# A leaner opening of an S4 and gMLP kernel: shorter table arithmetic, small transfers ahead of large ones, constant bf16 products on TensorE

## The chip, the core and the metric

The kernel runs on one core of a Trainium2 chip. The metric is the device time of one execution in microseconds (us). In the profile PE is TensorE (PEld its weight loads), DVE is VectorE, ACT is ScalarE, POOL is GpSimd and SP is SyncE.

## The reference

One token stream x of 2048 x 576 goes through two sublayers, each behind a layernorm that the conditioning vector c modulates:

```python
mod = (silu(c) @ w_mod).reshape(1, 6, 1, 576)   # w_mod: 576 x 3456
sa, ca, ga, sb, cb, gb = (mod[:, i] for i in range(6))
h = layernorm(x) * (1 + ca) + sa
x = x + ga * S4(h)
h = layernorm(x) * (1 + cb) + sb
x = x + gb * gMLP(h)
```

S4 is a long convolution, one per channel: dt = exp(log_dt), K[d, l] = Re(sum over n of C[d, n] dt B[d, n] exp(dt A[d, n] l)) for 576 channels, 128 states and 2048 positions, then y = conv(K, h) + h * Dskip. gMLP is z = gelu(h @ w_in) with 4608 columns, the second half layernormed and multiplied along the positions by w_sp (2048 x 2048, plus b_sp), the product of both halves times w_out.

## The kernel before, in words

`body` calls `ssm` (modulation, first layernorm, S4) and then the two phases of the MLP, whose start `ssm` also weaves in. The change concerns the first fifth of `ssm`.

Per pole (one channel and state) the kernel needs the logarithm of C B dt as a magnitude (`lw`) and a phase in turns (`ph`), the decay `al` = dt A_re, and the turns per position `tau` with its 64-fold `tau64`, both without their whole turns. `poles` makes these as tables: `p0` for the first 128 channels, 128 x 144 elements, and `p1` for the other 384 of its four groups, 128 x 432. Each of the five results is split into three bf16 parts (`split3`: two copies on ACT, two differences on DVE, into `pt`), which POOL's queue writes to DRAM (`pa_d`, `pb_d`). `poles_load` reads them back rearranged, so that the parts lie along the partitions: `lb` holds the parts of al and lw, `lc` and `la` those of tau, tau64 and ph. Against the constant matrix `sel` TensorE then makes exponents (`e_unit`: lb x sel into a double bank ps and a bank pk, exponentiated by ACT into `et`) and phases (`t_unit`: lc and la x sel into ps; DVE takes the absolute value and ACT two sines, into `ft`). `p_unit` multiplies both on DVE into `pg`, `kg_unit` multiplies the pieces of the kernel K on TensorE (evicted by ACT into `kab`), `k1_unit` takes a first step of the convolution's transform. These units run for g = 0, 1, 2, ..., 35.

Beside this stand the modulation and the layernorm. `mod_unit(k)` multiplies one of the six parts of w_mod with silu(c) (the tile `ec`): 6 small f32 products for each half of the columns into two banks, evicted by ACT into `mpart`; a product with a matrix of ones (a part of the tile `small`) sums the partial results and spreads them over all partitions. k = 2 gives `gar` (ga), k = 1 gives `cga` = (1 + ca) ga, k = 0 gives `sga` = sa ga, which goes through three bf16 copies `gsp` with two corrections on DVE between them. The w_mod parts arrive as `wm`, `k_a` and `k_b`. `ln_stats(i)` makes the mean and 1/std of one of four tiles of x (`ln_x`, four blocks of 128 rows each): tiles 0 and 1 by copies and squares with accumulation on ACT (into a junk tile `st1o`, sums in `nm` and `ss`), tiles 2 and 3 by BATCH_NORM_STATS2 on DVE (`bs`). `ln_rows(b)` centres and scales block b with cga and makes `rt`, a constant rotation times 1/std. `ln_half(k)`, for sixteen half pairs of blocks, multiplies rows by rotations and adds gsp x `cs` into four banks; ACT evicts these to `st1o`, and POOL stores them (`u_d`).

The order of everything is written by hand. Every instruction of every engine is issued through `Pin.call`, which pins it behind the one before on its engine; so nearly all rows of the profile have its line, L223. The table `ORDER` (L53 on) is a list of tokens: a letter for the unit and a number for its instance. The class `Steps` (L880) runs the tokens: the units are generators, and each token runs one to its next `yield`. B are set-up steps (B0 starts the p0 loads, B1 those of p1, B2 to B6 load c, sel, small, msk and dsk, B7 the first part of w_mod), O a step of p0, P a step of p1, M a step of a `mod_unit`, i, w loads of w_mod, j, x loads of ln_x, g, r, a loads of the rotations, S `ln_stats`, R `ln_rows`, A `ln_half`, Q `poles_load`, and e, t, p, k and 1 the units above. `PLAN` names the buffer of each use of the ring tiles: five of `et`, three of `ft`, four banks pk_a to pk_d, two double banks ps_a and ps_b, and so on. A bank pk has 512 f32 columns; the modulation and `ln_half` use 288 of them (HC), `kg_unit` and `k1_unit` 256.

## Time and profile before

| | |
|---|---|
| three runs | 1691.30, 1702.78, 1696.13 us; median 1696.13 |
| profiled execution | 1701.01 us, span 1698.9 |
| busy: PE, PEld | 1623.6 (96%), 1239.8 us |
| busy: DVE, ACT, POOL | 1298.9 (76%), 875.5 (52%), 210.6 us |
| mean granted TensorE clock | 0.98 of full speed |
| DMA | 380.61 MB, 224 GB/s over the span |

The span runs from the first to the last instruction of the record. A row of a timeline has a start, a duration, the engine, the operation, out<-in by the program's names, and in brackets the idle time ahead of it with what ended it. A row of the stretches has a window, its length and the busy time of each engine in it with the count of instructions. A row of the groups has the total busy time, the mean of one in ns, and the idle time ahead of them. PEclk is the TensorE clock that was granted, as a share of full speed; rows at half speed show 0.50.

### The profile page before, as it was taken

Reading aid. Unit: us, or ns where it says so; the run is one execution under the profiler, and the core shown is the slowest. Engines: PE = TensorE matmul, PEld = TensorE weight load, DVE = VectorE, ACT = ScalarE, POOL = GpSimd, SP = SyncE. Lnnn points to the kernel's source line nnn. Section 1 sums busy time; section 2 is a strip of 40 time slices with the busy share of each in tenths; the row PEclk is TensorE's granted clock in tenths of the full one; section 3 lists DMA queues with packets and bytes.
Section 4 is the critical chain, followed back from the end, with each engine's and each line's share of the span. In section 5 each row is a group of like instructions: output and inputs, shape, how many; then the busy total and the mean of one; then the engine's idle time right before and its main releaser. Section 6 shows DMA issues by size and latency. Waiting matters only on the chain.

```text
span 1698.9 us, 39926 instructions
## 1 busy us (share of the span) xinstructions
PE 1623.6 (96%) x16870; PEld 1239.8 (73%) x16870; DVE 1298.9 (76%) x2241; ACT 875.5 (52%) x1309; POOL 210.6 (12%) x340
## 2 busy tenths in 40 slices
...
GB/s 231 168 206 214 189 147 177 180 285 222 264 289 240 256 266 289 254 258 247 244 127 284 304 265 253 228 210 173 225 224 233 194 233 119 263 282 251 192 243 29
DMA packets 186386, 380.61 MB, mean 224 GB/s; under 512 B 38448, under 2 KB 105776, under 8 KB 185440
## 3 DMA queue, kind: packets, MB, share of 16 engines
...
q14 instruction: 46, 0.38, 0.1%
HBM read 272.73 MB, written 105.29 MB: 223 GB/s over the span
## 4 chain that ended last, share of the span: by engine, by line
PE 76%; DVE 6%; DMA 4%; issue 2%; ACT 2%; ACTq 0%; DVEq 0%; POOLq 0%
PE ps L223 53%; PE pz L223 13%; PE pk_b L223 3%; PE pk_a L223 2%; DMA zset<-set_d 2%; DVE zset L223 2%; PE pk_d L223 2%; PE pk_c L223 2%; DVE gt L223 1%; DMA wa_d<-zset 1%; PE pt L223 1%; PE ps_a L223 1%; DMA zz_a<-v_d 0%; PE ps_b L223 0%; DMA v_d<-v_b 0%
## 5 line engine op out<-in xcount | busy, mean ns | idle before, releaser
L223 PEld LDWEIGHTS <-zset 128*128 128x128 f16 x7182 | 702.1, 98 | 88.3 <-DMA zset<-set_d 3.6
L223 PE MATMUL ps<-wsp,zset 128*128 128x256 f16 x6048 | 667.0, 273 | 3.4 <-DMA zset<-set_d 2.2
L223 PE MATMUL pz<-wz,nt 128*128 128x512 f16 (+1 forms) x1120 | 220.6, 358 | 1.2 <-ACT nt L223 0.7
L223 ACT ACTIVATE z<-gt 128x1024 f16<-128x1024 f32 x56 | 59.0, 1054 | 252.6 <-DVE gt L223 252.6
L223 PEld LDWEIGHTS <-nt 128*128 128x128 f16 x1120 | 109.6, 98 | 106.3 <-ACT nt L223 0.9
L2190 POOL DMA_DIRECT2D zset<-set_d x96 | 51.0, 532 | 865.1 <-PE ps L223 593.0
L223 PE MATMUL ps<-wout,z 128*128 128x288 f16 x1092 | 138.3, 286 | 0.0
L223 DVE SCALAR_TENSOR_TENSOR gt<-ps,sc,bsp 128x512 f32<-128x512 f32 x36 | 27.0, 749 | 144.7 <-PE ps L223 143.0
L223 PEld LDWEIGHTS <-z 128*128 128x128 f16 x1176 | 115.1, 98 | 28.9
L223 DVE TENSOR_TENSOR raw<-raw 128x256 f32<-128x256 f32 (+3 forms) x238 | 126.8, 540 | 11.7 <-DMA raw<-z_d 6.7
L223 PE MATMUL ps<-n2o,zset 128*128 128x256 f16 x1134 | 128.2, 273 | 0.0
L223 DVE SCALAR_TENSOR_TENSOR gt<-ps,sc,gt 128x512 f32<-128x512 f32 (+1 forms) x180 | 122.2, 696 | 7.6
L223 ACT ACTIVATE zset<-raw 128x1792 f16<-128x1792 f32 x48 | 81.0, 1691 | 61.0 <-PE ps L223 26.6
L223 DVE TENSOR_TENSOR zset<-raw,zset 128x1792 f16<-128x1792 f32 x48 | 96.9, 2020 | 13.9 <-ACT zset L223 13.9
L223 DVE TENSOR_TENSOR z<-ps,z 128x512 f32<-128x512 f32 (+1 forms) x126 | 72.0, 599 | 31.9 <-ACT z L223 24.2
L223 ACT ACTIVATE z<-pz,sc 128x512 f32<-128x512 f32 (+1 forms) x96 | 52.0, 574 | 40.6 <-PE pz L223 33.9
L223 ACT ACTIVATE wsp<-raw,sc 128x1792 f16<-128x1792 f32 x25 | 44.5, 1784 | 46.2 <-DVE raw L223 40.2
L223 ACT ACTIVATE z<-z,sc 128x1024 f32<-128x1024 f32 x21 | 24.1, 1149 | 75.6 <-DVE z L223 71.9
L223 ACT ACTIVATE z1b<-gt 128x512 f16<-128x512 f32 (+1 forms) x22 | 17.7, 821 | 85.0 <-DVE gt L223 85.0
L223 PE MATMUL ps<-n2q,wf 128*128 128x512 f16 x252 | 55.7, 379 | 0.0
L223 DVE BATCH_NORM_STATS2 bsz<-z 128x6 f32<-128x384 f32 x96 | 48.5, 548 | 5.1 <-ACT z L223 4.7
L223 DVE SCALAR_TENSOR_TENSOR wsp<-raw,sc,wsp 128x1792 f16<-128x1792 f32 x25 | 52.0, 2078 | 0.3 <-ACT wsp L223 0.3
...
## 6 DMA issues: line engine op xcount, KB each, us to landing
...
```

What stands on the lines that cost most here:

```text
L223: return self.tc.keep_in_program_order(f(*a, **k))
L2190: self.nc.gpsimd.dma_start(o, self.set_d[f, j - 1] if j else self.wa_d[f])
```

## The change

It has five parts.

1. `poles` is written anew. It now gives ten short generators (tokens O0 to O9 and P0 to P9: step, turns, weights, log, ratio, second, angle and three splits). The four products of C and B are one operation of four widths, the two absolute values one of two widths, tau and tau64, and al and lw, are split together, and several pairs of passes are joined. On DVE one table has 31 instructions in place of 47. One DRAM tensor `p_d` takes the place of two, and two fixed `lb` tiles, cleared once at the start (B8), the place of new ones.
2. `ORDER` and `PLAN` of the opening are new: the p0 steps come first, POOL's queue has the writes of p0 and the loads lc, lb, la (tokens q0 to q2) ahead of the large w_mod parts, SP's has the A_re inputs last among the inputs of either table, dsk behind small and msk ahead of the w_mod parts that SP loads. From about the fifth `ln_half` on the token order is that of before.
3. `ln_stats` of tile 1 is on DVE instead of ACT.
4. `ln_rows` makes `rt` for two blocks in one operation, 8 of 128 columns in place of 16 of 64.
5. `warm` is new: products of a 128 x 128 bf16 constant with a bf16 constant of 512 - c0 columns into columns c0 on of a bank, which nobody reads. 88 of 512 columns stand ahead of the first `e_unit`; `mod_unit` has some ahead of its first half, between its halves and behind its ones-product; `ln_half` has 5 of 224 columns behind its second block, `kg_unit` and `k1_unit` 4 of 256 columns each for the first ten and nine g. In all they are 720 LDWEIGHTS and MATMUL pairs.

```diff
@@ the opening of ORDER: its first lines @@
-B0 O0 O0 O0 O0 B2 O0 O0 O0 O0 B7 O0 B1 O0 O0 O0 B6 O0 O0 O0 O0 O0 O0 x0 O0 O0 O0 O0 P0 S0 O0 S0 B3 O0 O0 i2 O0 O0 O0 P0 M2 O0 O0 S0 S0 B4 P0 S0 O0 Q0 P0 e1 S0 M2 e1 i1
+B0 B2 B8 O0 B1 x0 B3 B4 B6 B5 O1 O1 O1 O7 O2 O7 B7 O2 O7 P0 O2 O3 O2 O2 O7 O7 O1 O4 O6 O5 O4 O8 O6 O8 O6 O6 O8 O9 O8 O9 O8 O9 O9 O9 q0 q1 q2 i2 i1 i0 g0 g1 j1 P2 P2 P2
+S0 S0 S0 e1 e0 P2 P2 S0 S0 e1 e0 e1 e0 e1 e0 e2 e2 e2 e2 P1 P1 P1 P1 t1 M2 t0 P7 P3 P4 t1 S0 P7 P7 P4 t0 P5 P7 M2 t1 t0 M2 t2 M1 P6 P6 P6 P6 P7 t1 t0 t2 M2 t2 M1 t2 M1
...
+WARM_M = {0: (8, 20), 1: (18, 20), 2: (6, 8), 3: (0, 4), 4: (0, 4), 5: (0, 4)}
...
-        pa_d = dram.tile([4, 2, 9, CW // 2], BF, name="pa_d")
-        pb_d = dram.tile([4, 2, 6, CW // 2], BF, name="pb_d")
+        p_d = dram.tile([4, 2, 15, CW // 2], BF, name="p_d")
...
+        def poles(c0, c1, Q, order, own=None):
+            n, w = c1 - c0, 144 * (c1 - c0)
             f0, f1 = CW * c0, CW * c1
+            big = own or [ea.tile([128, 432 * k], F32, name="e%d" % k, bufs=1) for k in (10, 7)]
+            pt0 = []
+
+            def s(i, m=1):
+                i, t = (i, big[0]) if i < 10 else (i - 10, big[1])
+                return t[:, w * i:w * i + w * m]
+
+            def sm(i, m):
+                return s(i, m).rearrange("p (m f) -> p m f", m=m)
+
+            slot = {"log_dt": 0, "A_im": 1, "A_re": 3, "C_re": 6, "C_im": 7, "B_re": 8, "B_im": 9}
+            for k in order:
+                S.dma_start(s(slot[k]).rearrange("p (c f) -> p c f", c=n), I["A_" + k][f0:f1].rearrange("(c p f) -> p c f", p=128, f=144))
+            ldt, tau, tau64, al, lw, ph = (s(i) for i in range(6))
+            ax, ay, mx, mn, wr, wi, q1, q2, dt = (s(i) for i in range(6, 15))
+
+            def step():
                 A.activation(dt, ldt, AF.Exp)
                 yield
+
+            def turns():
+                V.scalar_tensor_tensor(tau, dt, 1.0 / (2 * math.pi), tau, op0=ALU.mult, op1=ALU.mult)
+                V.tensor_scalar(tau, tau, 2097152.0, -2097152.0, op0=ALU.min, op1=ALU.max)
+                yield
+                V.tensor_scalar(tau64, tau, MAGIC, MAGIC, op0=ALU.add, op1=ALU.subtract)
+                V.tensor_tensor(tau, tau, tau64, op=ALU.subtract)
+                yield
+                V.tensor_scalar(tau64, tau, MAGIC / 64, MAGIC / 64, op0=ALU.add, op1=ALU.subtract)
+                V.tensor_tensor(tau64, tau, tau64, op=ALU.subtract)
+                yield
                 V.tensor_tensor(al, dt, al, op=ALU.mult)
                 yield
+
+            def weights():
+                shape = [128, 2, 2, w]
+                V.tensor_tensor(s(10, 4).rearrange("p (b c f) -> p b c f", b=2, c=2), bc(sm(6, 2)[:, None], shape), bc(sm(8, 2)[:, :, None], shape), op=ALU.mult)
+                yield
+                V.tensor_tensor(wr, wr, q2, op=ALU.subtract)
+                V.tensor_tensor(wi, wi, q1, op=ALU.add)
+                yield
+                V.tensor_single_scalar(s(6, 2).bitcast(I32), s(10, 2).bitcast(I32), 0x7FFFFFFF, op=ALU.bitwise_and)
+                V.scalar_tensor_tensor(mx, ax, 1e-37, ay, op0=ALU.max, op1=ALU.max)
                 V.tensor_tensor(mn, ax, ay, op=ALU.min)
                 yield
+                V.reciprocal(q1, mx)
+                yield
+                V.tensor_tensor(mn, mn, q1, op=ALU.mult)
+                yield
+
+            def log():
                 A.activation(lw, mx, AF.Ln)
+                yield
+
+            def ratio():
+                A.activation(q2, mn, AF.Square)
+                A.activation(q2, q2, AF.Ln, bias=one)
+                yield
                 A.activation(ph, mn, AF.Arctan)
                 yield
+
+            def second():
+                V.scalar_tensor_tensor(lw, q2, 0.5, lw, op0=ALU.mult, op1=ALU.add)
+                V.tensor_tensor(lw, lw, ldt, op=ALU.add)
+                yield
+
+            def angle():
+                V.tensor_tensor(ax, ay, ax, op=ALU.is_gt)
+                V.tensor_scalar(ay, wr, 0.0, -0.5, op0=ALU.is_lt, op1=ALU.mult)
+                yield
+                V.scalar_tensor_tensor(ph, ax, -math.pi / 2, ph, op0=ALU.mult, op1=ALU.add)
+                V.tensor_single_scalar(ph.bitcast(I32), ph.bitcast(I32), 0x7FFFFFFF, op=ALU.bitwise_and)
+                yield
+                V.scalar_tensor_tensor(ph, ph, 1.0 / (2 * math.pi), ay, op0=ALU.mult, op1=ALU.add)
+                V.tensor_single_scalar(ph.bitcast(I32), ph.bitcast(I32), 0x7FFFFFFF, op=ALU.bitwise_and)
+                yield
+                V.scalar_tensor_tensor(ph.bitcast(I32), wi.bitcast(I32), -2147483648, ph.bitcast(I32), op0=ALU.bitwise_and, op1=ALU.bitwise_or)
+                V.scalar_tensor_tensor(ph, tau, 31.5, ph, op0=ALU.mult, op1=ALU.add)
+                yield
+
+            def split3(i, m, row, at):
+
+                if own is None or not pt0:
+                    pt0[:] = [eb.tile([128, 2592], BF, name="pt", bufs=1)]
+                at = 0 if own is None else 3 * w * at
+                pt = pt0[0][:, at:at + 3 * w * m].rearrange("p (m q f) -> p m q f", m=m, q=3)
+                src, q = sm(i, m), sm(15, m)
+                A.activation(pt[:, :, 0], src, AF.Copy)
+                yield
+                V.tensor_tensor(q, src, pt[:, :, 0], op=ALU.subtract)
+                yield
+                A.activation(pt[:, :, 1], q, AF.Copy)
+                yield
+                V.tensor_tensor(pt[:, :, 2], q, pt[:, :, 1], op=ALU.subtract)
+                yield
+                pq = pt.rearrange("p m q f -> p (m q) f")
+                for c in range(c0, c1):
+                    for h in range(2):
+                        Q.dma_start(p_d[c, h, row:row + 3 * m].rearrange("q (p f) -> p q f", p=64),
+                                    pq[64 * h:64 * h + 64, :, 144 * (c - c0):144 * (c - c0) + 144])
+                yield
+
+            return [step(), turns(), weights(), log(), ratio(), second(), angle(),
+                    split3(1, 2, 6, 0), split3(3, 2, 0, 2), split3(5, 1, 12, 4)]
 
...
-        def poles_load(c, Q):
-            for n, d_, k in (("lb", pb_d, 0), ("lc", pa_d, 0), ("la", pa_d, 3)):
-                t_ = tb.tile([112, 9, 128], BF, name=n)
-                if n == "lb":
-                    Q.memset(t_[32:64], 0.0)
+        def poles_load(c, Q, names=("lb", "lc", "la")):
+            for n in names:
+                k = {"lb": 0, "lc": 6, "la": 9}[n]
+                t_ = lbs[c % 2] if n == "lb" else tb.tile([112, 9, 128], BF, name=n)
                 for h in range(2):
-                    Q.dma_start(t_[64 * h:64 * h + 48], d_[c, h, k:k + 6].rearrange("q (c g n) -> (q c) g n", c=8, g=9))
+                    Q.dma_start(t_[64 * h:64 * h + 48], p_d[c, h, k:k + 6].rearrange("q (c g n) -> (q c) g n", c=8, g=9))
                 lt[n, c] = t_
...
+        unit = consts_s.bitcast(BF)[:, 5:6]
+
+        def warm(t, n, c0):
+            for _ in range(n):
+                T.matmul(t[:, c0:], bc(unit, [128, 128]), bc(unit, [128, 512 - c0]), start=True, stop=True, skip_group_check=True)
+
         def mod_unit(k):
             wm = wmt.pop(k)
             pm = [ps1(), ps1()]
+            warm(pm[0], WARM_M[k][0], 0)
             for hh in range(2):
+                if hh:
+                    warm(pm[0], WARM_M[k][1], HC)
                 for kt in range(6):
                     j = (kt + 2 * hh) % 4
                     T.matmul(pm[hh][32 * j:32 * j + 32, :HC], ec[:, kt:kt + 1].to_broadcast([96, 32]),
@@ -450,6 +448,7 @@
             pm = [ps1(), ps1()]
             for hh in range(2):
                 T.matmul(pm[hh][:, :HC], ones, mpart[:, HC * hh:HC * hh + HC], start=True, stop=True)
+            warm(pm[1], 4, HC)
             yield
...
-            if i < 2:
+            if i < 1:
...
-            rt = ep.tile([128, 64], F32, name="rt", bufs=4)
-            V.tensor_scalar(rt, r1t[b // 2][0][:, b % 2].rearrange("p r k -> p (r k)"), r[:, j:j + 1], None, op0=ALU.mult)
-            row[b] = n, rt, r1t[b // 2][1][:, b % 2].rearrange("p r k -> p (r k)")
+            if b // 2 not in rts:
+                rt = rts[b // 2] = ep.tile([128, 2, 64], F32, name="rt")
+                V.tensor_tensor(rt, r1t[b // 2][0].rearrange("p b r k -> p b (r k)"), bc(r[:, j - b % 2:j - b % 2 + 2][:, :, None], [128, 2, 64]), op=ALU.mult)
+            row[b] = n, rts[b // 2][:, b % 2], r1t[b // 2][1][:, b % 2].rearrange("p r k -> p (r k)")
             yield
...
+                if t:
+                    warm(pms[3], 5, HC)
...
+            if g == 1:
+                warm(pa[:, 0], 88, 0)
...
+            warm(pm, 4 if g < 10 else 0, 256)
...
+            warm(pm[1], 4 if g < 9 else 0, 256)
...
+                for i in range(2):
+                    lbs.append(tb.tile([112, 9, 128], BF, name="lb%d" % i, bufs=1))
+                    G.memset(lbs[i][32:64], 0.0)
...
-        many = {"O": lambda k: p0, "P": lambda k: p1, "M": mod_unit, "S": ln_stats, "R": ln_rows, "A": ln_half, "e": e_unit, "t": t_unit,
+        many = {"O": lambda k: p0[k], "P": lambda k: p1[k], "M": mod_unit, "S": ln_stats, "R": ln_rows, "A": ln_half, "e": e_unit, "t": t_unit,```

What the change moves, as each engine's order of instructions shows it. POOL's queue from its first transfer on, before (pt are the split parts, wm, k_a and k_b the parts of w_mod):

```order
L223 DMA pb_d<-pt 64x3x144 x2
L223 DMA pa_d<-pt 64x3x144 x4
L223 DMA pb_d<-pt 64x3x144 x2
L223 DMA wm<-in_w_mod 96x1728 x2
L223 DMA pa_d<-pt 64x3x144 x2
L223 MEMSET lb 32x1152
L223 DMA lb<-pb_d 48x1152 x2
L223 DMA lc<-pa_d 48x1152 x2
L223 DMA la<-pa_d 48x1152 x2
L223 DMA k_a<-in_w_mod 96x1728 x2
```

and the same place of the change:

```order
L224 MEMSET lb_124 32x1152
L224 MEMSET lb_126 32x1152
L224 DMA p_d<-pt 64x6x144 x4
L224 DMA p_d<-pt 64x3x144 x2
L224 DMA lc<-p_d 48x1152 x2
L224 DMA lb_124<-p_d 48x1152 x2
L224 DMA la<-p_d 48x1152 x2
L224 DMA wm<-in_w_mod 96x1728 x2
L224 DMA k_a<-in_w_mod 96x1728 x2
L224 DMA k_b<-in_w_mod 96x1728 x2
```

The five split results leave in three larger writes, nothing stands between them and the loads back, and all three w_mod parts follow behind.

ACT around the first exponents (et) and the first modulation part (mpart), before:

```order
L223 ACTIVATE mpart<-pk_a 128x288
L223 ACTIVATE mpart<-pk_b 128x288
L223 ACTIVATE et_b<-ps_a 128x1024
L223 ACTIVATE et_c<-ps_b 128x1024
L223 ACTIVATE et_b<-pk_c 128x512
L223 ACTIVATE et_c<-pk_d 128x512
L223 ACT_TABLE_LOAD
L223 ACTIVATE t_lw<-t_n_B_re 128x432
```

and after (e_129 and e_130 are the two wide tables of p1):

```order
L224 ACTIVATE et_d<-ps_a 128x1024
L224 ACTIVATE et_d<-pk_c 128x512
L224 ACTIVATE pt<-e_129 128x2x432
L224 ACT_TABLE_LOAD
L224 ACTIVATE e_129<-e_129 128x432
L224 ACTIVATE e_130<-e_129 128x432
L224 ACTIVATE e_130<-e_130,consts_s 128x432
L224 ACTIVATE pt<-e_130 128x2x432
L224 ACT_TABLE_LOAD
L224 ACTIVATE e_129<-e_129 128x432
L224 ACTIVATE mpart<-pk_d 128x288
L224 ACTIVATE mpart<-pk_a 128x288
```

The eviction of M2 stood ahead of the first exponents; it now stands behind six of their copies and behind the logarithms and the arctangent of p1.

PE from the ones-product of M2 to the products of M0, before:

```order
L223 MATMUL pk_a<-mpart,small 128x288
L223 MATMUL pk_b<-mpart,small 128x288
L223 MATMUL pk_c<-k_a,ec 32x288 x6
L223 MATMUL pk_d<-k_a,ec 32x288 x6
...
L223 MATMUL pk_c<-mpart,small 128x288
L223 MATMUL pk_d<-mpart,small 128x288
L223 MATMUL pk_a<-k_b,ec 32x288 x6
```

and after, from the products of M1 on (the rows of consts_s are the constant ones, each kind shown once: 18 of 512 columns ahead of the first half, 20 of 224 between the halves):

```order
L224 LDWEIGHTS consts_s
L224 MATMUL pk_a<-consts_s 128x512
L224 MATMUL pk_a<-k_a,ec 32x288 x6
...
L224 MATMUL pk_a<-consts_s 128x224
...
L224 MATMUL pk_d<-k_a,ec 32x288 x6
L224 MATMUL pk_b<-mpart,small 128x288
L224 MATMUL pk_c<-mpart,small 128x288
```

M1's second half and its ones-product stand behind 38 constant products on PE.

167 lines of the change are left out of this document (40 added, 127 removed).

## Prediction

> **What bounds the kernel now.** I read the stretches first: the busy time of each engine from the start of the record to four points of the opening, and over the rest. Columns: length, then busy time and instructions of PE, PEld, DVE, ACT, POOL, then the granted clock of PE, the DMA share and GB/s.
>
> ```profile
> 0.00:36.78 36.78, 8.70 (x45) 2.69 (x47) 26.67 (x85) 23.07 (x47) 16.24 (x31) 1.00 0.87 229
> 36.78:46.20 9.42, 8.83 (x56) 4.20 (x52) 6.00 (x9) 7.99 (x12) 0.54 (x1) 1.00 1.03 249
> 46.20:68.23 22.03, 17.95 (x322) 9.57 (x326) 20.10 (x35) 19.68 (x38) 8.00 (x13) 0.85 0.76 207
> 68.23:145.66 77.43, 59.42 (x1158) 29.90 (x1147) 70.95 (x140) 67.28 (x131) 30.54 (x47) 0.75 0.60 193
> 145.66:300.00 154.34, 146.16 (x3315) 102.67 (x3314) 140.91 (x179) 146.46 (x253) 21.56 (x36) 0.97 0.58 174
> 400.00:1699.00 1299.00, 1290.90 (x10463) 1023.92 (x10461) 960.11 (x1676) 547.47 (x720) 111.17 (x179) 1.00 0.69 231
> ```
>
> Three regimes are to be seen. Behind 400 us PE works 1290.90 of 1299.00 us: nothing edited at the front changes that, it only starts earlier or later. From 46.20 to 145.66 DVE is the fullest engine (20.10 of 22.03, then 70.95 of 77.43), with 6.5 us idle in the second stretch. Up to 46.20 nobody is full: a chain of small steps sets the time. So a change to the opening is worth what it takes from that chain, then from DVE's work, and from DVE's idle time.
>
> The timeline shows the chain. The table of the first 128 channels goes out to DRAM and returns rearranged before anything can be exponentiated:
>
> ```profile
> 3.24 0.31 DVE L223 TENSOR_TENSOR et_a<-t_dt,et_a 128x144 f32<-128x144 f32 x1 [2.30 <-DMA et_a<-in_A_A_im]
> 12.00 0.53 DVE L223 TENSOR_TENSOR t_sq<-et_a,pt 128x144 f32<-128x144 f32 x2 [1.42 <-ACT pt L223]
> 22.56 0.30 DVE L223 TENSOR_TENSOR pt<-t_sq,pt 128x144 bf16<-128x144 f32 x1
> ...
> 36.78 1.23 DVE L223 TENSOR_SCALAR ft_a<-ps_a 128x1024 int32<-128x1024 int32 x1 [0.79 <-PE ps_a L223]
> 46.20 0.45 DVE L223 SCALAR_TENSOR_TENSOR cga<-pk_c,gar 128x288 f32<-128x288 f32 x1
> 53.20 0.45 DVE L223 TENSOR_TENSOR sga<-pk_a,gar 128x288 f32<-128x288 f32 x1
> 67.49 0.82 DVE L223 SCALAR_TENSOR_TENSOR sga<-gsp,msk,sga 128x576 f32<-128x576 bf16 x1 [0.88 <-ACT gsp L223]
> ```
> ```profile
> 23.16 1.28 POOL L223 DMA_DIRECT2D pa_d<-pt  x2 [1.52 <-DVE nm L223]
> 25.82 1.03 POOL L223 DMA_DIRECT2D lb<-pb_d  x2 [0.29 <-POOL lb L223]
> 29.27 1.00 POOL L223 DMA_DIRECT2D la<-pa_d  x2 [1.43 <-DMA pa_d<-pt]
> ```
> ```profile
> 30.51 0.61 PE L223 MATMUL ps_a<-sel,lb 48*128 48x512 bf16 x2
> 35.43 0.39 PE L223 MATMUL ps_a<-sel,la 48*128 48x256 bf16 x1 [1.00 <-DMA la<-pa_d]
> 38.30 1.33 PE L223 MATMUL pk_a<-mpart,small 128*128 128x288 f32 x2
> 42.87 1.16 PE L223 MATMUL pk_d<-k_a,ec 96*32 96x288 f32 x12 [0.57 <-ACT mpart L223]
> ```
>
> The last table part is ready at 22.9, its write is issued at 23.16, and PE takes the returned la at 35.43: 12.3 us later. Beside it runs the modulation chain (matmul, eviction into mpart, ones-product, then cga and sga), and the first normalised rows (A0) follow its last sum at 68.3.
>
> Last, PE's clock. The same view over windows of 3.41 us, on which the clock changes:
>
> ```profile
> 62.30:65.71 3.41, 3.41 (x66) 1.59 (x62) 3.41 (x5) 3.32 (x12) 0.90 (x2) 0.50 0.62 149
> 65.71:69.12 3.41, 3.41 (x120) 2.47 (x113) 2.50 (x6) 3.41 (x7) 0.00 (x0) 1.00 1.02 264
> 69.12:72.53 3.41, 1.36 (x29) 0.52 (x24) 3.27 (x6) 3.29 (x8) 0.00 (x0) 1.00 0.15 34
> 72.53:75.95 3.42, 3.41 (x18) 1.14 (x17) 1.99 (x5) 2.53 (x7) 0.00 (x0) 0.50 0.02 5
> ```
>
> After the window with 1.36 us of work the next runs at 0.50; after 62.30, filled to 3.41, the clock is back at 1.00. The stretch of 77.43 us has a mean clock of 0.75: half of it at half speed.
>
> **The change part by part.** Prices, from the groups by shape and the page:
>
> ```profile
> L223 DVE TENSOR_TENSOR pt<-t_sq,pt 128x432 bf16<-128x432 f32 x5 | 2.8, 602 | 0.0
> L223 DVE TENSOR_TENSOR pt<-t_sq,pt 128x144 bf16<-128x144 f32 x5 | 1.4, 303 | 0.3 <-ACT pt L223 0.3
> L223 DVE RECIPROCAL t_rnd<-t_n_B_re 128x432 f32<-128x432 f32 x1 | 2.9, 2853 | 0.0
> L223 DVE RECIPROCAL t_rnd<-et_a 128x144 f32<-128x144 f32 x1 | 1.1, 1054 | 0.0
> L223 DVE TENSOR_SCALAR t_n_C_im<-t_ph 128x432 f32<-128x432 f32 x2 | 0.8, 384 | 0.1
> L223 DVE TENSOR_SCALAR et_a<-et_a 128x144 f32<-128x144 f32 x3 | 0.7, 233 | 0.1
> L223 DVE TENSOR_SCALAR rt<-r1t,r 128x64 f32<-128x64 f32 x16 | 4.1, 257 | 0.0
> L223 DVE BATCH_NORM_STATS2 bs<-ln_x 128x6 f32<-128x288 f32 x16 | 6.3, 434 | 0.6 <-DMA ln_x<-in_x 0.6
> ```
> ```profile
> L223 PE MATMUL ps<-n2q,wf 128*128 128x512 f16 x252 | 55.7, 379 | 0.0
> ```
>
> *Tables.* From 144 to 432 columns a two-operand pass grows from 0.30 to 0.60 us, so about 0.16 fixed and 1.0 ns a column; a one-operand pass 0.5 ns. Before, 34 two-operand passes, 12 one-operand, one reciprocal: for the wide table 34 x 0.60 + 12 x 0.38 + 2.85 = 27.8 us, for the first 14.4. After, 23 (one of four widths, four of two), 7 (one of two) and the reciprocal: 1.9 + 4 x 1.04 + 18 x 0.60 + 2.9 + 2.85 = 22.7, and 10.9. DVE saves 5.1 + 3.5. The eight wide rt against 16 save some 1.7 (128 columns at about 0.29 for two of 0.257). Against it, the statistics of the second tile come from ACT to DVE: 8 x 0.434 = 3.5 plus four aggregates, near 3.6 net of the two small passes that go. Net -6.7 of DVE's time; -5 is the other end, if only the issue pitch of wide passes counts. ACT loses about 8.
>
> *Return of the first table.* It starts at 3.24, works 10.9 and waits at least about 1.8 (the 1.42 on ACT's pt stays, and a short wait for an input): ready at 15.9 instead of 22.9. With the same 12.3 us behind it la is back at 28.3, or 27 since POOL no longer has a memset and a w_mod load in between; lb, 4.7 us from issue to PE in the rows above, at about 25. So ft_a can start near 29.2, against 36.78: 7.5 us of lead for the exponentials and angles.
>
> *Constant products at the front.* 88 of 128 x 512 stand ahead of the first exponents. 55.7 us for 252 is 0.221 each at full clock; the pitch at half clock is near 0.42. With the first one or two windows at half clock they take 21 to 23 us and end at 21 to 24, before lb is back: nothing is queued behind them but products that wait for lb. Cost nothing; if lb came at 20 they would cost up to 4.
>
> *Constant products in the modulation.* These are not covered. PE's order is fixed, so the 18 + 20 ahead of and inside M1's 12 real products stand before its eviction, its ones-product and cga. By columns, 0.221 x 224 / 512 is 0.097. M1: 18 x 0.221 + 20 x 0.097 = 5.9 us. M0: 8 x 0.221 + 20 x 0.097 + 4 behind M1's ones = 4.1. M2's 6 and 8 lie under lb's return.
>
> *Order.* M2's eviction now stands on ACT behind the exponent copies and the table's logarithms.
>
> ```profile
> 31.16 1.02 ACT L223 ACTIVATE et_b<-ps_a 128x1024 f32<-128x1024 f32 x1
> ...
> 34.10 1.28 ACT L223 ACT_TABLE_LOAD   x1
> 35.39 0.56 ACT L223 ACTIVATE t_lw<-t_n_B_re 128x432 f32<-128x432 f32 x1
> ```
>
> Three such copies, three of half the width (about 0.6), two table loads and six passes of 432 columns or twice that (0.56 to 0.9) are some 11 us from lb's first product on, about 25.8: its ones-product comes near 37.5, as in the trace (38.30). From there: 1.25 ones, fillers and a phase product to 40.2; 4.0; 1.16; 2.0; 1.16; 0.5 eviction; 1.25 ones: cga at 50 against 46.20. DVE, which has 7.5 us of lead, then idles some 6 before it. M0 follows: 2.2, 1.16, 2.0, 1.16, 0.9 of exponents, an eviction that two ACT copies precede: sga at about 61 against 53.20. In before the second gsp sum came 14 us behind sga since tables were queued between; in after it can follow in 7: 68.4, against 68.3. **A0 stays within a microsecond or two of where it was.** The saved 6.7 us on DVE is spent waiting for cga and sga.
>
> *Behind A0* the order of the work is nearly the same. The waits of DVE in the stretch 68.23 to 145.66:
>
> ```profile
> DVE ss L223 <- ACT st1o_b L223: 1.4, 1, 1.4
> DVE ft_c L223 <- PE ps_a L223: 1.1, 1, 1.1
> DVE pg_b L223 <- PE pk_a L223: 0.6, 1, 0.6
> ```
>
> The wait for ACT's statistics goes (-1.4); of the 1.7 that DVE waits for PE here, half goes if the constant products hold the clock (-0.85; bounds 0 and -1.7); 0.8 us more table work is left there: -1.45. The products inside the halves, kg and k1 units take 16 x 5 x 0.097 = 7.8, and some 8 more, of PE time that stood idle (77.43 - 59.42 = 18.0); an eviction of a tile waits for the fillers in its own bank, 0.4 us each, while matmuls at half clock, half of this stretch, go twice as fast. From 145.66 to 300 PE is busy 146.16 of 154.34 us at a mean clock of 0.97: 0.03 x 146.16 = 4.4 us too many. DVE and ACT are as full there, so I put half on the path: -2.2 (bounds 0 and -4.4).
>
> *Sum:* 0 - 1.45 - 2.2 = **-3.6 us**. The profiled execution took 1701.0 us, span 1698.9 and 2.1 around it: 1697.4. The runs shown have the median 1696.1: **1692.5**.
>
> **The rivals.**
>
> (1) *The lead carries through.* If w_mod's k_a lands later than I think, or the phases cover it, M1's 5.9 us are no delay, and DVE goes on without idling at cga. To 145.66 DVE then has 26.67 + 6.00 + 20.10 + 70.95 = 123.7, less 5, and the idle that cannot go, about 10.7: 129.4 against 145.7, -16: 1680. For it: DVE is the fullest engine from 46.20 on. Against: PE's fixed order.
>
> (2) *The clock falls ahead of M1.* PE idles some 2 us before M2's ones-product; the clock fell after the row 69.12, with 1.36 of 3.41 busy. M1's and M0's fillers then run at half clock for two to three windows, 3.4 to 5.1 us lost twice over, part of it hidden: A0 7.5 later, some 2.5 of it won back by the lighter DVE: +5, 1701, slower than before by a little. It decides once sga comes later than 61.5.
>
> (3) *The products do not lift the clock* (the change doesn't do what it says). 88 x 0.42 = 37 us: the first exponents wait until 38 instead of 30.51, M1's 38 take 11, M0's 8: +20, 1716. Against: the rows 62.30 and 65.71, where a filled window was followed by full clock.
>
> (4) *The clock is not on the path.* DVE is full at 0.75 clock, so the half-clock products lay beside it: no gain but the 1.4 less 0.8, -0.6, so 1695.5. For it: only 1.7 us of DVE's larger waits there name PE.
>
> [...]
>
> **How the numbers follow.** The forecast, 1692.5, has 0.40 (own range 1688 to 1697). Rival 1 has 0.22, rival 2 0.16, rival 3 0.04, rival 4 0.18. The range 1678 to 1703 takes in 1680 and 1701 with a margin for the medians (1691.3 to 1702.8 before) and leaves out rival 3 and the far edge of rival 1. A measurement of this kernel can tell about 1%, 17 us: below 1679 lies some 0.6 of rival 1 and a little of the forecast, 0.16; above 1713 rival 3, 0.04; between them 0.80.
>
> **What would show it.** Right: ft_a's first pass near 29, cga near 50 with DVE idle before it, sga near 61, A0's first product at 69 to 71, clock 1.00 nearly throughout from 68 to 146, the statistics' wait gone. A cga at 46 or sooner makes rival 1; a row at 0.50 between 36 and 55 with sga past 62 rival 2; first exponents past 35 rival 3; full clock in 68 to 146 with the same length of it rival 4. The forecast is wrong if A0 moves by more than 4 us either way.

## The result and the profile after

The changed kernel takes 1708.03 us (median of 9 runs, 1705.39 to 1713.79); the kernel before beside it 1696.52 (9 runs, 1691.3 to 1702.78). The ratio is 1.0064, with a 95% interval of 1.0047 to 1.0081: some 11 us slower, where the prediction had 4 us faster. That is inside the 1% that the prediction took a measurement of this kernel to tell, but the whole interval lies above 1. The profiled execution took 1708.31 us, span 1706.5, against 1701.01 and 1698.9. The mean clock rose to 0.988 from 0.981, and PE executes 360 more matmuls (17230 for 16870): the constant products are 360 pairs, and the 720 of part 5 counts both halves of a pair.

The same stretches as in the prediction, with the same columns:

```profile
0.00:36.78 36.78, 32.57 (x159) 13.21 (x159) 26.48 (x67) 27.13 (x47) 15.41 (x29) 0.91 0.86 233
36.78:46.20 9.42, 7.86 (x52) 3.93 (x53) 8.23 (x13) 7.62 (x11) 1.35 (x2) 1.00 1.01 248
46.20:68.23 22.03, 18.02 (x234) 11.18 (x232) 11.37 (x17) 8.57 (x15) 2.60 (x4) 0.92 0.31 93
68.23:145.66 77.43, 67.82 (x1282) 39.41 (x1282) 64.11 (x128) 60.29 (x115) 23.70 (x38) 0.93 0.65 188
145.66:300.00 154.34, 148.03 (x3253) 102.48 (x3253) 139.99 (x177) 144.34 (x252) 21.18 (x35) 0.97 0.58 176
400.00:1699.00 1299.00, 1294.77 (x10484) 1024.96 (x10483) 962.58 (x1675) 549.52 (x724) 113.21 (x182) 1.00 0.69 232
```

Up to 36.78 DVE runs 67 instructions where it ran 85, and the clock from 68.23 to 145.66 rose from 0.75 to 0.93. Yet from 46.20 to 68.23 DVE works only 11.37 us where it worked 20.10, and ACT 8.57 for 19.68. The loss is there. (For the kernel before, the clock column is no guide up to 46.20. It says 1.00, while a ones-product takes 1.33 us at 38.30 and 0.75 at 44.94, so its rows show half speed first and full speed later.) DVE's timeline shows the steps:

```profile
29.90 1.23 DVE L224 TENSOR_SCALAR ft_a<-ps_b 128x1024 int32<-128x1024 int32 x1 [2.03 <-PE ps_b L224]
50.05 0.46 DVE L224 SCALAR_TENSOR_TENSOR cga<-pk_b,gar 128x288 f32<-128x288 f32 x1 [4.80 <-PE pk_b L224]
61.02 0.46 DVE L224 TENSOR_TENSOR sga<-pk_b,gar 128x288 f32<-128x288 f32 x1 [4.95 <-PE pk_b L224]
68.97 0.81 DVE L224 SCALAR_TENSOR_TENSOR sga<-gsp,msk,sga 128x576 f32<-128x576 bf16 x1
155.28 1.21 DVE L224 SCALAR_TENSOR_TENSOR ft_a<-ft_a,ps_a 128x1024 f32<-128x1024 f32 x1
403.15 0.69 DVE L224 TENSOR_TENSOR nt<-pt,nt 128x512 f16<-128x512 f32 x1 [1.64 <-ACT nt L224]
```

Phases start 6.9 us sooner (29.90 for 36.78). Then DVE waits 4.80 us for the product behind cga and 4.95 for the one behind sga, and cga and sga are 3.9 and 7.8 us late. The two last rows are places that both kernels pass with the same instruction; before they stand here, with the first product of A0:

```profile
145.66 1.21 DVE L223 SCALAR_TENSOR_TENSOR ft_a<-ft_a,ps_a 128x1024 f32<-128x1024 f32 x1
394.75 0.69 DVE L223 TENSOR_TENSOR nt<-pt,nt 128x512 f16<-128x512 f32 x1 [2.40 <-ACT nt L223]
```
```profile
69.65 0.30 PE L223 MATMUL pk_b<-gsp,cs 32*64 32x288 bf16 x1
```

PE's timeline of the change holds the constant products (consts_s) and what stands behind them:

```profile
0.97 21.16 PE L224 MATMUL ps_a<-consts_s 128*128 128x512 bf16 x88 [0.97 <-DVE consts_s L187]
24.06 0.87 PE L224 MATMUL ps_a<-sel,lb 48*128 48x512 bf16 x2 [1.94 <-DMA lb<-p_d]
37.34 0.75 PE L224 MATMUL pk_b<-mpart,small 128*128 128x288 f32 x2 [1.05 <-ACT mpart L224]
40.95 4.11 PE L224 MATMUL pk_a<-consts_s 128*128 128x512 bf16 x18
46.09 2.15 PE L224 MATMUL pk_a<-consts_s 128*128 128x224 bf16 x20
50.82 1.91 PE L224 MATMUL pk_a<-consts_s 128*128 128x512 bf16 x8
53.76 2.15 PE L224 MATMUL pk_a<-consts_s 128*128 128x224 bf16 x20
59.66 1.33 PE L224 MATMUL pk_b<-mpart,small 128*128 128x288 f32 x2 [2.12 <-ACT mpart L224]
72.03 1.53 PE L224 MATMUL pk_d<-wm,ec 96*32 96x288 f32 x12
80.02 0.30 PE L224 MATMUL pk_b<-gsp,cs 32*64 32x288 bf16 x1
```

The 88 at the front end at 22.13, before lb lands, since PE then waits 1.94 us for it. The 18 + 20 of M1 and 8 + 20 of M0 take 10.3 us, and A0 is at 80.02 for 69.65. That lag of 10.4 us is 9.6 at the common pass (155.28 for 145.66), 8.4 at the first nt, and 7.6 in the spans.

### The profile page after: what moved, and what is told of

Read it like the earlier page. It is cut to its first block, busy times and chain, and to the rows that moved or that the text cites. A ratio compares the mean times of both kernels' runs of the same rounds, so it can differ in the third digit from the quotient of the medians.

```text
span 1706.5 us, 40549 instructions
## 1 busy us (share of the span) xinstructions
PE 1666.8 (98%) x17230; PEld 1268.1 (74%) x17230; DVE 1295.0 (76%) x2212; ACT 869.8 (51%) x1285; POOL 199.2 (12%) x322
## 4 chain that ended last, share of the span: by engine, by line
PE 84%; DVE 5%; DMA 4%; issue 3%; ACT 2%; POOL 0%; SPq 0%; ACTq 0%; DVEq 0%; POOLq 0%
PE ps L224 58%; PE pz L224 13%; PE pk_a L224 3%; PE pk_b L224 3%; PE pk_d L224 3%; PE pk_c L224 3%; DMA zset<-set_d 1%; DVE zset L224 1%; DMA u_d<-st1o_b 1%; PE ps_b L224 1%; DMA v_d<-v_b 1%; DVE gt L224 1%; PE ps_a L224 1%; ACT L224 1%; PE pt L224 1%
## 5 line engine op out<-in xcount | busy, mean ns | idle before, releaser
L224 PEld LDWEIGHTS <-zset 128*128 128x128 f16 x7182 | 702.0, 98 | 87.6 <-DMA zset<-set_d 2.8
L224 PE MATMUL ps<-wsp,zset 128*128 128x256 f16 x6048 | 666.7, 273 | 3.0 <-DMA zset<-set_d 2.1
L224 PE MATMUL pz<-wz,nt 128*128 128x512 f16 (+1 forms) x1120 | 220.6, 358 | 1.2 <-ACT nt L224 0.7
L224 PEld LDWEIGHTS <-nt 128*128 128x128 f16 x1120 | 109.5, 98 | 106.5 <-ACT nt L224 0.9
L224 ACT ACTIVATE z<-gt 128x1024 f16<-128x1024 f32 x56 | 59.0, 1054 | 248.4 <-DVE gt L224 248.4
L224 PE MATMUL ps<-wout,z 128*128 128x288 f16 x1092 | 138.4, 287 | 0.0
L224 PEld LDWEIGHTS <-z 128*128 128x128 f16 x1176 | 115.0, 98 | 28.9
L224 DVE SCALAR_TENSOR_TENSOR gt<-ps,sc,bsp 128x512 f32<-128x512 f32 x36 | 27.0, 749 | 143.2 <-PE ps L224 141.5
L224 DVE TENSOR_TENSOR raw<-raw 128x256 f32<-128x256 f32 (+3 forms) x238 | 126.8, 539 | 9.8 <-DMA raw<-z_d 4.9
L224 PE MATMUL ps<-n2o,zset 128*128 128x256 f16 x1134 | 128.2, 273 | 0.0
L224 DVE SCALAR_TENSOR_TENSOR gt<-ps,sc,gt 128x512 f32<-128x512 f32 (+1 forms) x180 | 122.2, 696 | 7.6
L224 ACT ACTIVATE zset<-raw 128x1792 f16<-128x1792 f32 x48 | 81.2, 1691 | 60.6 <-PE ps L224 25.2
L224 DVE TENSOR_TENSOR zset<-raw,zset 128x1792 f16<-128x1792 f32 x48 | 97.0, 2020 | 15.6 <-ACT zset L224 15.6
L224 DVE TENSOR_TENSOR z<-ps,z 128x512 f32<-128x512 f32 (+1 forms) x126 | 72.0, 599 | 31.9 <-ACT z L224 25.9
L224 ACT ACTIVATE z<-pz,sc 128x512 f32<-128x512 f32 (+1 forms) x96 | 51.7, 574 | 38.7 <-PE pz L224 31.2
L224 ACT ACTIVATE wsp<-raw,sc 128x1792 f16<-128x1792 f32 x25 | 44.5, 1784 | 46.1 <-DVE raw L224 41.9
L224 ACT ACTIVATE z<-z,sc 128x1024 f32<-128x1024 f32 x21 | 24.1, 1149 | 76.2 <-DVE z L224 72.5
L224 ACT ACTIVATE z1b<-gt 128x512 f16<-128x512 f32 (+1 forms) x22 | 17.7, 821 | 84.6 <-DVE gt L224 84.6
L224 PEld LDWEIGHTS <-consts_s 128*128 128x128 bf16 x360 | 33.6, 104 | 31.8 <-issue 15.2
L224 PE MATMUL ps<-n2q,wf 128*128 128x512 f16 x252 | 55.7, 380 | 0.0
L224 DVE SCALAR_TENSOR_TENSOR wsp<-raw,sc,wsp 128x1792 f16<-128x1792 f32 x25 | 52.0, 2078 | 0.3 <-ACT wsp L224 0.3
```

Source lines behind the costliest of these rows:

```text
L224: return self.tc.keep_in_program_order(f(*a, **k))
```

## The experiments

Each was timed in 5 rounds beside the kernel before; differences between two of them go by their ratios. The effects are of some us, so a single trace needs care: the profiled execution of the front products alone was 9 us quicker than its own median, that of the new opening with the products in the units alone 6 us slower, and that of the kernel before (1701.01) 4.5 us slower than the median of its nine runs. The expectations name their theories by letters of their round; the words ahead of each group say what was in question.

### Which products cost

In question: do the constant products carry the loss, and which of the three groups, or does the new order behind A0? First without any.

```diff
-            for _ in range(n):
+            for _ in range(0):
```

> The changed kernel without any of the constant products; tables, order and transfers as changed. Theory M (the products in M0 to M2 are the cost: they hold back cga and sga and with them everything queued on PE, ACT and DVE): cga near 46, sga near 52, DVE idle between 46 and 68 us falls from 10.7 to under 4, time 9 to 12 us below the changed kernel, about 1698. Theory O (the new order of the opening is the cost, the products are neutral): cga and sga come sooner, but the 7 us of DVE idle behind 70 us stay, 1705 to 1708. Theory C (the products' clock is worth more than they cost): half clock back in 46 to 150 us and slower than the changed kernel, 1711 or more.

1697.92 us, ratio 1.0013 (1.0002 to 1.0024): nearly all of the loss goes. Its DVE rows and its PE row at the places shown above:

```profile
45.79 0.46 DVE L224 SCALAR_TENSOR_TENSOR cga<-pk_b,gar 128x288 f32<-128x288 f32 x1 [2.20 <-PE pk_b L224]
51.28 0.46 DVE L224 TENSOR_TENSOR sga<-pk_b,gar 128x288 f32<-128x288 f32 x1
58.42 0.81 DVE L224 SCALAR_TENSOR_TENSOR sga<-gsp,msk,sga 128x576 f32<-128x576 bf16 x1
```
```profile
69.93 0.30 PE L224 MATMUL pk_b<-gsp,cs 32*64 32x288 bf16 x1
```

sga comes 9.7 us sooner than with the products, and A0 10.1: what PE's rows count for M1 and M0 (4.11 + 2.15 + 1.91 + 2.15 = 10.3). But the row of the second gsp sum says something else too. It stands at 58.42, 9 us sooner than in the kernel before, and A0 is where it was.

Without the products in the modulation, without those in the units (`ln_half`, `kg_unit`, `k1_unit`), and without the 88 at the front:

```diff
-WARM_M = {0: (8, 20), 1: (18, 20), 2: (6, 8), 3: (0, 4), 4: (0, 4), 5: (0, 4)}
+WARM_M = {k: (0, 0) for k in range(6)}
...
-            warm(pm[1], 4, HC)
+            warm(pm[1], 0, HC)
```

> Without the constant products of the modulation alone; the 88 at the front and those of the halves, kg and k1 units stay. Theory M: as without all, 9 to 12 us below the changed kernel, about 1698, or a little less as the others still lift the clock. Theory O: 1705 to 1708. Theory U (the products inside the units are the cost, since the evictions wait for them): 1707.

```diff
-                    warm(pms[3], 5, HC)
+                    warm(pms[3], 0, HC)
...
-            warm(pm, 4 if g < 10 else 0, 256)
+            warm(pm, 0, 256)
...
-            warm(pm[1], 4 if g < 9 else 0, 256)
+            warm(pm[1], 0, 256)
```

> Without the constant products of the halves, kg and k1 units; those of the front and the modulation stay. Theory M: cga at 50 and sga at 61 as in the changed kernel, 1706 to 1710. Theory U: the DVE idle behind 70 us, 13.4 in the changed kernel, falls to about 7, 1701. Theory C: the clock falls again behind 70 us and it costs 3 or more, 1711.

```diff
-                warm(pa[:, 0], 88, 0)
+                warm(pa[:, 0], 0, 0)
```

> Without the 88 constant products at the front alone. Theory M and O: the first exponents and phases run at half clock as they do in the changed kernel (24.8 to 31.6 us), time within 2 us of the changed kernel. Theory C: the first table's products are later, 2 to 4 us slower.

1701.9 us, 1.0038 (1.0024 to 1.0051) without those of the modulation, A0 at 71.29; 1712.23, 1.0097 (1.0081 to 1.0112) without those of the units; 1712.35, 1.0094 (1.0077 to 1.011) without the front, A0 at 81.51. When one group is taken from the whole, only the modulation's products turn out to cost, 4 us; the other two help some 5 us each there. The next runs put single groups on bases without the others.

```diff
# the kernel before, with the calls of warm in mod_unit alone
+            warm(pm[0], WARM_M[k][0], 0)
...
+                    warm(pm[0], WARM_M[k][1], HC)
```

> The kernel before, with the constant products of the modulation alone added as the change has them. Theory M (each microsecond of these products delays cga and sga and the end by itself): cga at 51 to 53, sga at 62 to 64, 8 to 11 us slower than before, 1706. Rival (in the old order other work covers them, the harm needs the new order): under 4 us slower, 1700.

1702.7 us, 1.0049 (1.0031 to 1.0067): in the old opening as well the modulation's products cost, 8 us; A0 at 73.82.

```diff
# the changed kernel: front and modulation empty, units kept
+WARM_M = {k: (0, 0) for k in range(6)}
...
+            warm(pm[1], 0, HC)
...
+                warm(pa[:, 0], 0, 0)
```

> The changed kernel with the constant products of the halves, kg and k1 units alone; none at the front, none in the modulation. Theory M (modulation products cost some 6 us, unit products are worth up to 5): cga at 46 as without any, full clock from 60 to 150 us, 1692 to 1695, faster than both kernels. Rival Q (the half clock behind 70 us is not on the path once the modulation is quick): 1697 to 1699, as without any.

```diff
# the kernel before, with the calls of warm in ln_half, kg_unit and k1_unit alone
+                    warm(pms[3], 5, HC)
...
+            warm(pm, 4 if g < 10 else 0, 256)
...
+            warm(pm[1], 4 if g < 9 else 0, 256)
```

> The kernel before with the constant products of the halves, kg and k1 units added and nothing else. Theory M: half clock from 68 to 150 us falls from 44 us to under 15, 3 to 5 us faster than before, 1692. Rival Q: within 1.5 us of before; slower by 2 or more if the evictions' wait for the products costs.

1698.56 us, 0.9997 (0.998 to 1.0015), and 1699.09, 1.0006 (0.999 to 1.0022). The first of them also prices the modulation's products on a base without the front: 1.0094 with them against 0.9997 without is 16 us, with A0 12.0 us later (81.51 for 69.47). Of the second run, the stretch in which the kernel before has a clock of 0.75:

```profile
68.23:145.66 77.43, 65.56 (x1289) 36.84 (x1287) 69.33 (x138) 66.86 (x131) 29.73 (x46) 0.91 0.60 188
```

The clock is lifted to 0.91 with the old order, and the time does not move beyond its interval. The interval (0.999 to 1.0022) leaves a net gain of 0.1% at most, with the cost of the products (A0 comes 2.0 us later) and the gain of the clock in one. No run separates the two.

The front products alone, and the units' with those of M2 alone (which stand ahead of a wait of PE for ACT):

```diff
# the edits of the runs without modulation and without unit products, together
+WARM_M = {k: (0, 0) for k in range(6)}
...
+                    warm(pms[3], 0, HC)
```

> The changed kernel with the 88 products at the front alone. Theory F (they end before the first table is back, PE idles, the clock falls, and the next full windows come later than without them): half clock until some 52 us instead of 40.7, cga at 48, sga at 55 to 56, 3 to 5 us slower than the kernel without any products, 1.003 to 1.004 of before. Rival (they cost and bring nothing, as their stretch holds no other PE work): cga at 46 and 1.001 of before.

```diff
# the changed kernel: front empty, units kept
+WARM_M = {k: (6, 8) if k == 2 else (0, 0) for k in range(6)}
...
+            warm(pm[1], 0, HC)
...
+                warm(pa[:, 0], 0, 0)
```

> The changed kernel with the unit products and, in the modulation, only the 14 of part 2, which lie in PE's wait for ACT. Theory F: with them the clock is back by 32 us, cga at 45, sga at 51, where 47.0 and 54.2 stand with the unit products alone. If the opening's lead counted, 3 us faster than before, 0.998; by what the light opening (0.998 at 19 us less DVE work) showed, 0.999 to 1.000.

1707.28 us, 1.0056 (1.0036 to 1.0075), and 1701.25, 1.0027 (1.0012 to 1.0041). So the front's 88 cost some 7 us on a base without other products (1.0056 against 1.0013) and help 5 with the modulation's: the groups do not add up. M2's 14 cost some 5 (1.0027 against 0.9997), and the clock that was expected of them by 32 us came but did not stay: M2's second half took 1.16 us at 33.36, where with the units' alone it took 2.13 at 31.26, and from 36.78 to 46.20 the clock was 0.53, with cga at 47.24.

Why the front alone costs this much stays open. Its trace, of its quickest execution (1698.3 us), looks like the explanation that was expected: PE waits for lb (0.30 us) and then for ACT (1.93 us), the clock falls (512 columns from lb take 0.39 us at 24.33 and 0.61 at 27.41), and M1's ones-product still runs at half speed, where without any products it was at full speed; sga comes at 54.95 for 51.28, and A0 at 73.29 for 69.93. But the same product runs at half speed with the units' products alone, where nothing stands at the front. The three rows, of the runs without products, with the front's and with the units':

```profile
45.00 0.75 PE L224 MATMUL pk_b<-mpart,small 128*128 128x288 f32 x2 [1.98 <-ACT mpart L224]
46.18 1.33 PE L224 MATMUL pk_b<-mpart,small 128*128 128x288 f32 x2 [1.23 <-ACT mpart L224]
45.60 1.33 PE L224 MATMUL pk_b<-mpart,small 128*128 128x288 f32 x2 [0.77 <-ACT mpart L224]
```

So a late return of the clock is not the front's alone, and one trace of each cannot price it. The five executions of the front's run without a trace have mean clocks of 0.974 to 0.977 and take 1706.1 to 1711.0 us; the traced one has 0.981.

Last of this group, the products of M1 and M0 doubled, which should cost as much again if the delay is their own time:

```diff
-WARM_M = {0: (8, 20), 1: (18, 20), 2: (6, 8), 3: (0, 4), 4: (0, 4), 5: (0, 4)}
+WARM_M = {0: (16, 40), 1: (36, 40), 2: (6, 8), 3: (0, 4), 4: (0, 4), 5: (0, 4)}
```

> The changed kernel with the constant products of modulation parts 1 and 0 doubled (some 10 us more of PE ahead of cga and sga). Theory L (later cga and sga are paid in full): cga at 56, sga at 71, 8 to 10 us slower than the changed kernel, 1717. Rival (their clock pays part of it back): under 4 us slower, 1711.

1718.73 us, 1.0116 (1.0096 to 1.0136). DVE's waits for cga and sga grow from 4.80 and 4.95 us to 10.41 and 8.10:

```profile
55.71 0.46 DVE L224 SCALAR_TENSOR_TENSOR cga<-pk_b,gar 128x288 f32<-128x288 f32 x1 [10.41 <-PE pk_b L224]
69.84 0.46 DVE L224 TENSOR_TENSOR sga<-pk_b,gar 128x288 f32<-128x288 f32 x1 [8.10 <-PE pk_b L224]
```

Against the changed kernel sga moved by 8.8 us, A0 by 7.3 (87.34), the time by 8.8 (1.0116 against 1.0064), for 10.3 us more of products. The delay is the products' own time, less some that lies beside other waits.

### Whether the order behind A0 costs

In question: do the statistics of the second tile, now on DVE, or the fourth `mod_unit`, stand in the way once A0 is late?

```diff
# a part of ORDER
-e3 k2 A0 A0 P8 t5 S1 A0 A0 A0 A0 P8 S1 t3 M3 A1 A1 r2 t5 A0 S1 A1 S1 A1 t3 S1 R4
+e3 k2 A0 A0 S1 S1 S1 S1 P8 t5 A0 A0 A0 A0 P8 t3 M3 A1 A1 r2 t5 A0 A1 A1 t3 S1 R4
```

> The changed kernel with one edit of the order: the four steps of the second tile's statistics on DVE stand ahead of the last difference of the second p1 split instead of behind it, where DVE idles 3.7 us for ACT's copy. Theory O (the order leaves DVE idle behind the modulation, and this idle is on the path): the 3.7 us are filled, the point where before and change meet again (155.3 us in the changed kernel) comes 3 to 4 us sooner, about 1704. Theory P (PE or ACT set the end of that stretch, not DVE): the idle reappears at a later wait, 1707 to 1708.

```diff
# two parts of ORDER; the plan of the banks pk follows the new order
-R6 M4 p5 w5 S2 12 M4 k3 e8 M4 e7 k3 M4 e8 A4
+R6 p5 S2 12 k3 e8 e7 k3 e8 A4
...
-p4 A5 t7 a4 A4 M4 A5 t6 A6 A6 A6 p4 A6 t6
+p4 A5 M4 t7 a4 M4 A4 M4 A5 t6 M4 w5 A6 A6 A6 p4 A6 M4 t6
```

> The changed kernel with modulation part 4 (needed only by the MLP) some 40 steps later in the order, behind the sixth half: its two evictions and its ones-product no longer stand on ACT ahead of the sine for which DVE waits 4.0 us at 106 to 110 us. Theory O: that wait falls below 1.5 us and the time by 2 to 4 us, about 1705. Theory P: another wait takes its place, 1707 to 1708.

1708.24 us, 1.007 (1.0048 to 1.0091), and 1710.44, 1.0091 (1.0063 to 1.0118): neither move gains. With the statistics early the common pass was 1.5 us sooner, at 153.76, and the first nt at 405.17 was later again. Nor did the move earn the 1.5 us: A0 stood at 77.67 there and at 80.02 in the change, though no token ahead of it differs. The clock from 69.17 to 72.58 was 1.00 in the one execution and 0.54 in the other. So the place of A0 differs by some 2 us between executions of one order. Both moves without the modulation's products:

```diff
# the edits of the two above, and
+WARM_M = {k: (0, 0) for k in range(6)}
```

> The changed kernel without the modulation's constant products and with both moves (statistics early, part 4 late); front and unit products stay. Theories M and O together: 1701.9 of the kernel without modulation products, less 4 to 7: 1695 to 1698, level with or a little below the kernel before (1696.5). Theory P: no better than 1701.

1705.18 us, 1.0051 (1.0032 to 1.0071), against 1.0038 without the moves. So these two places in the order do not carry the loss; that the whole new order costs little by itself was shown by the run without any products (1.0013). Parts 3 and 4 of the change on the kernel before:

```diff
-            if i < 2:
+            if i < 1:
...
# ln_rows as in the change: rt for two blocks at once
```

> The kernel before with two parts of the change alone: the second tile's statistics on DVE instead of ACT, and rt for two blocks in one operation. DVE has 2 us more, ACT 8 us less. If DVE is the bound from 68 to 146 us: 1 to 2 us slower. If ACT's order is part of the bound: 1 to 4 us faster.

1701.32 us, 1.0023 (1.0009 to 1.0038): no gain, but a loss of some 4 us. Here the statistics fall among the steps of the modulation, and the second gsp sum is at 69.73.

### What DVE's and ACT's work is worth

The prediction took DVE for the bound from 46.20 to 145.66. In question: what does the end gain when DVE has less to do? On the kernel before, first without the sixteen passes of `ln_rows` that centre the rows and scale them by cga, then without the statistics of the second tile:

```diff
-                V.scalar_tensor_tensor(n, n, nm[:, j:j + 1], cga, op0=ALU.add, op1=ALU.mult)
```

> The kernel before without the sixteen passes on DVE that centre and scale the rows of x with cga (16 x 0.81 = 12.9 us of DVE); the rows go into the rotation as loaded, so this part of the computation is left out. If DVE's work sets the length of the opening, as the forecast took it: 9 to 13 us faster. If the three engines bound each other through their orders: less than half of that, 2 to 6 us.

```diff
+            if i == 1:
+                lns[i] = lns[0]
+                return
```

> The kernel before without the statistics of the second tile of x (the first tile's are used for both, so this part of the computation is left out): ACT 8 us less, DVE 2.2 us less, nothing added anywhere. Theory A: 4 to 8 us faster. Theory D: within 1.5 us of before.

1698.29 us, 1.0006 (0.9991 to 1.0021), though DVE was busy 11.5 us less (1287.4 for 1298.9 in the whole execution); and 1696.43, 0.9995 (0.9981 to 1.0008), with ACT busy 5.9 us less (869.6 for 875.5). The first of them in the stretch, and on DVE's timeline:

```profile
68.23:145.66 77.43, 60.90 (x1168) 32.00 (x1158) 63.69 (x129) 68.64 (x135) 30.46 (x47) 0.73 0.62 194
```
```profile
142.89 1.22 DVE L223 SCALAR_TENSOR_TENSOR ft_a<-ft_a,ps_a 128x1024 f32<-128x1024 f32 x1 [1.77 <-ACT ft_a L223]
171.31 1.23 DVE L223 TENSOR_TENSOR pg_a<-et_a,ft_b 128x1024 f32<-128x1024 f32 x1 [1.54 <-ACT et_a L223]
```

DVE works 63.69 us of the stretch for 70.95, the common pass is 2.8 us sooner, and ahead of it and of a later product DVE waits for ACT, 1.77 and 1.54 us. This later product starts at 171.31, and in the kernel before at 171.52: the lead is gone. The opposite direction, twenty evictions of ACT's on DVE:

```diff
+COPIED = {(g, 0) for g in range(20)}
```

> The kernel before, with one of the two evictions of the first twenty k1 units on DVE instead of ACT: some 7 us of ACT's work moves to DVE between 60 and 230 us. Theory A (ACT, with its evictions, paces the stretch from 70 to 300 us, 95% busy in its second part): 2 to 5 us faster. Theory D (what is won ahead of 300 us is lost at a later wait that does not move): within 1.5 us of before. If DVE paces: 3 us slower.

1711.34 us, 1.0072 (1.0053 to 1.0091). One group of five of those copies:

```profile
L223 DVE COPY k_a<-pk_c 128x256 f32<-128x256 f32 x5 | 2.1, 422 | 7.6 <-PE pk_a L223 3.1 <-PE pk_d L223 2.4 <-ACT kab_a L223 2.1
```

Five copies work 2.1 us, and DVE stands idle 7.6 us just ahead of them, while its other work is queued behind. What is light on DVE is not free when its place in the order waits for another engine. How much of the 12 us is the copies' own work and how much such waits was not separated. Last, everything together: the new opening with the units' products alone, without those statistics and those passes.

```diff
# the edits of the new opening with unit products, of the two kernels above, together
+                lns[i] = lns[0]
...
-                V.scalar_tensor_tensor(n, n, nm[:, j:j + 1], cga, op0=ALU.add, op1=ALU.mult)
```

> The changed kernel with the unit products only, and with two parts of the computation left out: the statistics of the second tile of x (the first tile's serve both) and the sixteen passes that scale the rows with cga. Full clock, DVE 19 us lighter than in the kernel without products. If the three engines pace each other between 60 and 150 us: the point 145.7 of before comes 8 to 12 us sooner and the time is 1686 to 1690. Theory D: the point comes sooner, but the time stays within 3 us of before.

1695.7 us, 0.9982 (0.9969 to 0.9994): 3 us. The stretch, and a row in which its lead goes:

```profile
68.23:145.66 77.43, 66.08 (x1261) 37.39 (x1261) 53.19 (x96) 60.91 (x117) 25.10 (x40) 0.91 0.69 207
```
```profile
124.03 1.22 DVE L224 TENSOR_SCALAR ft_c<-ps_a 128x1024 int32<-128x1024 int32 x1 [7.25 <-PE ps_a L224]
```

DVE works 53.19 us there for 70.95, ACT 60.91 for 67.28, the clock is 0.91 for 0.75. The last pass of pg_a ahead of this row starts at 113.66 and in the kernel before at 117.86, 4.2 us later; behind the wait of 7.25 us for PE the kernel is 1.1 us late (124.03 for 122.89). A light DVE waits for PE instead. The units' products are in this run too, so a part of PE's work in that wait is theirs.

### All runs by the place of A0

Shift of A0's first product, of the common pass, of the first nt and of the time against the kernel before, in the profiled execution of each, and of the median (ratio less 1, times 1697), in us:

| kernel | A0 | pass | nt | profiled time | median |
|---|---|---|---|---|---|
| new opening, unit products | -0.2 | +0.2 | +5.4 | +3.6 | -0.5 |
| no products | +0.3 | -0.6 | -3.0 | -4.2 | +2 |
| units and M2 | +0.6 | +3.2 | +1.6 | -0.8 | +5 |
| no modulation products | +1.6 | +1.7 | -2.9 | -3.6 | +6 |
| before, unit products | +2.0 | +3.0 | +2.0 | +0.2 | +1 |
| front products only | +3.6 | +1.4 | -5.2 | -2.7 | +10 |
| before, modulation products | +4.2 | +3.0 | -0.2 | +1.2 | +8 |
| no unit products | +8.4 | +13.2 | +9.6 | +8.7 | +16 |
| the change | +10.4 | +9.6 | +8.4 | +7.3 | +11 |
| no front products | +11.9 | +16.4 | +12.8 | +12.0 | +16 |
| modulation products doubled | +17.7 | +22.2 | +19.7 | +18.0 | +20 |
| statistics early | +8.0 | +8.1 | +10.4 | +9.1 | +12 |
| part 4 of the modulation late | +10.5 | +14.2 | +18.8 | +18.6 | +15 |
| both moves, no modulation products | +0.5 | +8.1 | +7.4 | +6.2 | +9 |
| before, copies on DVE | +4.1 | +7.7 | +13.4 | +13.0 | +12 |
| before, statistics and rt of the change | +1.6 | +1.0 | +3.8 | +2.8 | +4 |
| before, no row passes | +0.1 | -2.8 | +0.2 | -2.6 | +1 |
| before, no second statistics | -2.1 | -6.2 | -2.9 | -6.0 | -1 |
| light opening | -0.3 | +0.9 | -4.0 | -5.5 | -3 |

The first eleven differ in their products alone or in the new opening and its products, ordered by A0. The common pass follows A0 within 5 us, and the profiled time follows the first nt within some 3 us in every row. A shift of A0 by 8 us or more reaches the end. What becomes of 4 us and less is hidden by the spread between executions: with the modulation's products on the kernel before, A0 was 4.2 us late in the traced execution and the first nt 0.2 early. The medians lie mostly up to 8 us above the shift of A0. The traced execution of the kernel before, 4.5 us slower than its median, may account for a part of that; the rest is not explained. The next five move work between engines or in the order. Two of them lose 9 and 4 us though A0 is at most 1.6 us late: both moves without the modulation's products, and the statistics and rt on the kernel before. The last three have lighter engines and end within 3 us of the kernel before by their medians. No kernel with the work complete was measured to beat it: the best, the new opening with the units' products, equals it.

## Why the prediction was wrong

*The start held.* Phases at 29.90 (29.2 forecast), M2's ones-product at 37.34 (37.5), cga at 50.05 (50), sga at 61.02 (61), the second gsp sum at 68.97 (68.4). So the uncovered products were costed rightly, and rivals 1 and 3 fell: the lead did not carry (cga at 50.05), and the clock was lifted (the 88 took 21.16 us and not 37, and from 68.23 to 145.66 it was 0.93 for 0.75). Only M2's products lay elsewhere than forecast: not under lb's return (24.06) but at 29.72 and 33.26, ahead of a wait of 1.05 us for ACT.

*The step that failed is the 0 of the sum: "A0 stays within a microsecond or two of where it was."* It took A0 to follow the last gsp sum, as it did before by 1.3 us from the end of that sum. After, the sum ends at 69.78 and A0 starts at 80.02, 10.2 us later. In the new order the last products of a k unit, then M3, e3, e5, k2 and t5 stand between on PE, and the k unit needs et_c, which DVE makes behind sga, just ahead of that last sum. DVE's rows behind sga (61.02), and the row with which PE goes on:

```profile
63.83 2.35 DVE L224 TENSOR_TENSOR pg_b<-et_c,ft_b 128x1024 f32<-128x1024 f32 x2
...
68.37 0.68 DVE L224 TENSOR_TENSOR et_c<-ft_b,et_c 128x512 f32<-128x512 f32 x1
68.97 0.81 DVE L224 SCALAR_TENSOR_TENSOR sga<-gsp,msk,sga 128x576 f32<-128x576 bf16 x1
```
```profile
69.10 0.32 PE L224 MATMUL pk_b<-et_c,pg_b 128*32 128x64 f32 x8 [1.80 <-DVE et_c L224]
```

So PE, too, is held until DVE is past sga, and then has 10.9 us of work before A0 without a gap, the products of M3 (72.03) among it; 2.8 us of it are constant products (at 70.53, 73.50, 76.48 and 78.28). In the kernel before those of M3 ran from 61.03 on, beside the gsp steps:

```profile
61.03 1.65 PE L223 MATMUL pk_b<-wm,ec 96*32 96x288 f32 x10
```

I looked when A0's input is ready, not what stands ahead of A0 in its queue and what that waits for. The run without products shows the same from the other side: with the sum at 58.42, the k unit goes on at 58.55 and A0 comes 11.4 us later, at 69.93. There the shortening of the sum by 9 us only made good the work that the new order puts behind it.

*The premise behind it was wrong too.* "From 46.20 to 145.66 DVE is the fullest engine", so its saved work was to pay for the wait. The saving itself was smaller than the 6.7 us (5 at the least) that were worked out: DVE's busy time fell by 3.9 us, from 1298.9 to 1295.0. And the run without row passes shows that less work of DVE's earned nothing at the end: 11.5 us less of it moved the end by +1 us, between -1.5 and +3.6 by its interval. By the rows shown DVE, ACT and PE wait for each other in turn, and a lead of one is lost at its next wait for another. What paces the stretch from A0 to 300 us is only argued from these waits; no run isolates it.

*The other terms of the sum were near in the trace.* From 68 to 146 I had -1.45, and the lag went from 10.4 to 9.6, -0.8; from 146 to 395 -2.2, measured -1.2. That the clock earned these was not shown. With the old order the units' products and their clock earned nothing together (1.0006), as rival 4 had it; in the changed kernel taking them away cost some 5 us (1.0097 against 1.0064).

*Rival 2* came nearest with +5 and the right side, but its mechanism did not: the products of M1 and M0 ran at full clock (4.11 us for 18 of 512 columns is 0.228 each), and sga came at 61.02, ahead of its 61.5. In these two units only M0's ones-products and the four constant ones behind them ran at half clock (1.33 us at 59.66, against 0.75 at 37.34). The range ended at 1703, 5 us short, as the delay at A0 had no bound of its own in the sum: with +10 there it is -3.6 + 10.4 = +6.8 on the profiled 1701.0, so 1707.8, and 1708.31 was measured. On the medians the same addition does not close: 1692.5 + 10.4 is 1702.9 against 1708.03, and these 5 us stay open.
